# Batch 0's head of an attention-plus-MLP kernel in a new order: score halves of pairs 0 and 1 in a row, 54 narrow blank matmuls for six wide ones, and the first part of w_in loaded in two halves

## The chip, the cores and the metric

The kernel runs on one core of one Trainium2 chip. The metric is the device time of one execution in microseconds, taken as the median of three runs. The profile of the kernel before comes from one further execution.

## The reference, cut to what matters

```python
# q, k, v: (4 batches, 8 heads, 768 positions, 64)
k_sum = k.reshape(B, H, 24, 32, D).max(axis=3)        # one key per block of 32
v_sum = v.reshape(B, H, 24, 32, D).mean(axis=3)
scores_l = where(|i - j| < 16, q @ k.T / 8, -1e9)     # local window
scores_s = q @ k_sum.T / 8 + log(32)                  # 24 block summaries
a = softmax(concat([scores_l, scores_s], -1))
x = (a @ concat([v, v_sum], 2)).transpose(0, 2, 1, 3).reshape(3072, 512)
h = x @ w_in                                          # 512 x 2048
out = (h * sigmoid(beta * h)) @ w_out                 # 2048 x 512
```

## The kernel before, in words

The work goes batch by batch (B = 4). Within a batch the eight heads are four pairs g = 0 to 3, since two heads of 64 fill the 128 partitions. Attention of a pair runs in two halves u = 0, 1 of 384 positions: scores into PSUM, exponential on ScalarE, product with the values, division on VectorE, transposition to xT. Then comes the MLP: sixteen 128-row tiles of h = w_in.T x, SiLU on ScalarE, and the product with w_out. Attention of batch b + 1 is woven into the output product of batch b, so only batch 0's attention has no matrix work beside it. This is the **head**, and the change is there.

Every engine executes its instructions in the order of the program, and nothing reorders them. For the head that order is the list HEAD, one entry per step, read from left to right; a step puts instructions on one engine. The names:

- `blank n w`: n matmuls of zeros, w columns wide, each with its own 128x128 weight load, result unused (line 737).
- `kt g x`, `qt g x`: sixteen transpositions of pair g's keys or queries from the loaded rows into PSUM bank x (line 384; banks 0 to 5 are the halves of big0, big1, big2, banks 6 and 7 are one0 and one1). `kc g e`, `qc g e`: the copy to SBUF by engine e (a ScalarE, d VectorE, p GpSimd; the helpers are lines 368, 371 and 374).
- `km g`: maximum over key blocks on VectorE (line 361).
- `vc g e`: cast of the loaded values vst to ve (line 456); for pair 3 in two pieces. `vl`, `vu`: the lower and upper parts of the shifted copy vo. `sm x g..`: block means of the values by matmul (line 473); `mc g e`: their copy to vm_one.
- `sc g u bg`: the scores of pair g, half u, into big tile bg (lines 415 to 426, 18 matmuls). `ex g u`: their exponential on ScalarE (line 447).
- `av g x`: the product of half 0 with the values (lines 519 and 525); `no g`: division (lines 537, 538); `xt g x` and `xc g e`: transposition (line 545) and copy to xT.
- `wi i`: the load of columns 512 i to 512 i + 511 of w_in, cast on the way, issued by GpSimd (line 331). `begin p lo hi`: for h tiles 2p and 2p + 1 the matmuls of the contraction blocks lo to hi - 1 (line 578). `silu`: ScalarE's table switch.

Behind the head comes `main`, a list of steps of TensorE with side steps at positions given by the table AT: `h_two` finishes the h tiles of half 0, `av_two` does half 1 of the value product (line 511), eight GpSimd copies `v_odd` (lines 463, 464) fill the rest of vo, then GpSimd issues the loads of batch 1's keys, w_out (four parts) and batch 1's queries. VectorE scales w_out by 1/beta as its parts land (line 337).

Loads of batch 0: the keys and queries come in six pieces through GpSimd's queue (line 195). The values of pair 0 are loaded at once by SyncE; those of pairs 1 to 3 (line 216) wait until the third piece of keys has landed. Matmuls of line 384, 415 and so on are each preceded by a weight load in the same instruction stream.

Of the kernel before, what the change touches and what calls it, by code (L numbers as in the profile page):

```python
# [81 lines left out]
}  # L82

HEAD = [
# [12 lines left out]
]  # L97

FIRST = [('k', 0, 2), ('k', 2, 4), ('k', 4, 8), ('q', 0, 2), ('q', 2, 4), ('q', 4, 8)]
# [3 lines left out]
def kernel(  # L103
# [10 lines left out]
    nc = tc.nc  # L114
# [25 lines left out]
    k1 = d_model // P  # L140
# [73 lines left out]
    def load_v0(g):  # L214
        src = pair(v, 0, g)
        return nc.sync.dma_start(out=vst[g][:], in_=bass.AP(src.tensor, src.offset - W * D,
                                                            [[D, P], [P * D, JV], [1, D]]))

    def behind(a, b):
        tc.add_manual_dep(a.ins, b.ins.name,  # L220
                          mybir.DependencyInfo(mybir.DependencyClass.Sync, mybir.DependencyReason.DATA),
                          reason="order of loads")
# [8 lines left out]
    blank = head.tile([P, 512], bf16, name="blank")  # L231
# [27 lines left out]
    km = [const.tile([P, P], bf16, name=f"km{g}") for g in range(G)]  # L259
# [26 lines left out]
    vl = [None] + [load_v0(g) for g in range(1, G)]  # L286
# [28 lines left out]
    w_in_sb = const.tile([P, k1, d_ff], bf16, name="w_in_sb")  # L315
# [11 lines left out]

    w_in_r = moe_w_in.rearrange("(a p) n -> p a n", p=P)
    w_out_r = moe_w_out.rearrange("(a p) n -> p a n", p=P)
    def load_w_in(lo, hi):  # L330
        return nc.gpsimd.dma_start(out=w_in_sb[:, :, lo:hi], in_=w_in_r[:, :, lo:hi])

    def load_w_out(i, n=4):
        return nc.gpsimd.dma_start(out=w_out_sb[:, n * i:n * i + n], in_=w_out_r[:, n * i:n * i + n])
# [477 lines left out]
        cp(*a)  # L812

    def w_in_part(i):
        x = load_w_in(512 * i, 512 * i + 512)
        if i == 0 and HOLD[2] is not None:
            behind(x, (vl[1:] + rows0)[HOLD[2]])

# [2 lines left out]
            "ex": lambda g, u: weigh(0, g, u), "vc": lambda g, e, lo=0, hi=JV: v_cast(eng_of(e), g, lo, hi),  # L821
            "vu": upper, "vl": lower, "av": av0, "no": lambda g: norm(0, g, turns.pop(("o", g)), [0]),
            "xt": x0, "xc": x_copy, "wi": w_in_part, "silu": silu_table, "begin": begin}
    for name, *args in HEAD:
        STEP[name](*args)
# [145 lines left out]
```

## Time and profile before

| what | value |
|---|---|
| three runs | 209.53, 209.86, 211.06 us; median 209.86 |
| profiled execution: its time, its span | 210.59 us, 208.9 us |
| TensorE matmul busy | 200.0 us, 96% of the span |
| VectorE, ScalarE, GpSimd busy | 138.8, 124.9, 61.5 us |
| DMA | 34.12 MB, mean 163 GB/s |
| first h matmul (line 578) | 25.84 us after the span's start |

The span runs from the first to the last instruction; 1.69 us of the profiled execution lie around it. PE is TensorE's matmul row and PEld its weight loads, which overlap. In a row of the timeline stand the start, the busy time of the group, engine, line, operation, tiles and count, and in brackets how long the engine had been idle and what ended that. `issue` means that the profile shows nothing that the engine waited for.

### The profile page before, as it was taken

The page shows a single profiled execution, that of the slowest core. Times are in us where ns is not written, and L with a number is a line of the kernel's source. Part 1 is how long each engine was busy: PE and PEld are TensorE (multiplying, and loading weights), DVE is VectorE, ACT ScalarE, POOL GpSimd, SP SyncE. Part 2 cuts the span into 40 slices and gives each one's busy share as a digit, 9 for nine tenths or more (in the row PEclk, how much of TensorE's full clock was granted, in tenths as well). Part 3 has the DMA queues.
Part 4 walks back from the last instruction along what each step waited for, and adds up shares of the span by engine and source line. Part 5 has one row for each costly group of instructions (what it writes and reads, how often), then busy time and mean ns, then how long its engine had stood idle before and what let it go on. Part 6 is the DMA issues. An engine that isn't in the chain of part 4 may idle for free.

```text
span 208.9 us, 5772 instructions
## 1 busy us (share of the span) xinstructions
PE 200.0 (96%) x2383; PEld 138.9 (67%) x2387; DVE 138.8 (66%) x314; ACT 124.9 (60%) x189; POOL 61.5 (29%) x95
## 2 busy tenths in 40 slices
PE   7887899999999999999999999999999999999993
PEld 2476666665555675666888975667888856668882
DVE  4496674599999982868999621999889304464132
ACT  2365876679678212966979238768894439662210
POOL 7706991101530017422520162452501100000011
PEclk9999999999999999999999999999999999999998
DMA  5997999999958999999779979999936820000242
GB/s 114 188 221 124 167 208 207 206 207 222 184 139 222 218 246 260 225 188 209 148 173 250 199 213 285 205 192 202 122 126 66 189 100 3 0 0 3 100 100 100
DMA packets 79193, 34.12 MB, mean 163 GB/s; under 512 B 61488, under 2 KB 76224, under 8 KB 79168
## 3 DMA queue, kind: packets, MB, share of 16 engines
q1 hardware_dynamic: 61968, 23.92, 54.9%
q0 software_dynamic: 7424, 7.34, 22.0%
q10 hardware_dynamic: 9776, 2.50, 8.8%
q8 instruction: 18, 0.29, 0.6%
q14 instruction: 7, 0.06, 0.1%
HBM read 27.37 MB, written 6.29 MB: 161 GB/s over the span
## 4 chain that ended last, share of the span: by engine, by line
PE 78%; DMA 10%; DVE 6%; issue 2%; ACT 2%; POOL 1%; POOLq 0%
PE big L600 28%; PE one L664 16%; PE acc L664 12%; PE big L578 5%; DMA vst<-in_v_dram 4%; DMA w_in_sb<-in_moe_w_in_dram 4%; PE one L584 3%; DMA krow<-in_k_dram 3%; PE one L615 3%; PE one L600 2%; PE big L436 2%; PE big L511 2%; PE big L584 2%; PE big L384 1%; DVE xn L538 1%
## 5 line engine op out<-in xcount | busy, mean ns | idle before, releaser
L600 PE MATMUL big<-xT,w_in_sb 128*128 128x384 bf16 x360 | 60.5, 326 | 0.0
L600 PEld LDWEIGHTS <-w_in_sb 128*128 128x128 bf16 x384 | 37.6, 98 | 25.1 <-issue 0.7
L611 ACT ACTIVATE h_sb<-big,beta_sb 128x768 bf16<-128x768 f32 x45 | 39.6, 905 | 24.0 <-PE big L600 23.9
L664 PEld LDWEIGHTS <-h_sb 128*128 128x128 bf16 x320 | 30.6, 98 | 4.6 <-issue 0.2
L645 POOL TENSOR_TENSOR o_sb<-p,u 128x256 f32<-128x256 f32 x10 | 7.3, 728 | 84.8 <-DVE u L645 74.4
L447 ACT ACTIVATE e<-big,bias 128x768 bf16<-128x768 f32 x32 | 27.4, 900 | 6.7 <-PE big L426 4.3
L664 PE MATMUL one<-w_out_sb,h_sb 128*128 128x256 bf16 x240 | 30.4, 273 | 0.2 <-DVE u L645 0.2
L664 PEld LDWEIGHTS <-s_sb 128*128 128x128 bf16 x240 | 23.1, 98 | 3.3 <-issue 0.5
L645 DVE TENSOR_TENSOR s_sb<-h_sb 128x768 bf16<-128x768 bf16 (+2 forms) x16 | 7.8, 488 | 23.7 <-ACT h_sb L611 23.6
L645 DVE TENSOR_TENSOR u<-one,p 128x256 f32<-128x256 f32 x20 | 8.4, 419 | 17.4 <-PE one L664 17.4
L456 POOL CAST ve<-vst 128x832 bf16<-128x832 f32 (+2 forms) x16 | 14.5, 914 | 17.9 <-DMA vst<-in_v_dram 14.9
L615 PE MATMUL one<-w_out_sb,h_sb 128*128 128x512 bf16 x61 | 14.5, 380 | 0.4 <-issue 0.3
L451 DVE TENSOR_TENSOR e<-e,mask 128x768 bf16<-128x768 bf16 x24 | 14.1, 618 | 0.4 <-ACT e L447 0.2
L368 ACT COPY o_sb<-one 128x256 f32<-128x256 f32 (+1 forms) x14 | 6.1, 433 | 12.9 <-PE one L664 7.1
L365 POOL COPY kw<-km 128x288 bf16<-128x288 bf16 x12 | 6.4, 534 | 22.5 <-DVE km L357 12.2
L361 DVE TENSOR_REDUCE km<-kT 128x24 bf16<-128x768 bf16 x12 | 11.3, 944 | 2.1 <-ACT kT L368 2.1
L538 DVE TENSOR_TENSOR xn<-big,r 128x768 bf16<-128x768 f32 x12 | 11.5, 957 | 0.4
L578 PE MATMUL big<-xT,w_in_sb 128*128 128x384 bf16 x64 | 11.4, 326 | 0.3 <-DMA w_in_sb<-in_moe_w_in_dram 0.3
L664 PE MATMUL acc<-t_sb,h_sb 128*128 128x256 bf16 x80 | 10.9, 273 | 0.0
L368 ACT COPY p<-acc 128x256 f32<-128x256 f32 x10 | 3.8, 376 | 11.6 <-PE acc L664 7.3
L664 PE MATMUL one<-t_sb,s_sb 128*128 128x256 bf16 x80 | 10.4, 273 | 0.2 <-ACT o_sb L368 0.2
L831 ACT ACTIVATE h_sb<-big,beta_sb 128x384 bf16<-128x384 f32 x16 | 8.3, 578 | 3.7 <-PE big L578 3.7
(145 smaller groups left out, 315.0 us busy)
## 6 DMA issues: line engine op xcount, KB each, us to landing
out_dram<-o_sb SPq DMA_DIRECT2D x19, 256.0 KB, 3.5
vst<-in_v_dram SPq DMA_DIRECT2D x13, 336.0 KB, 5.2
kst<-in_k_dram SPq DMA_DIRECT2D x8, 384.0 KB, 4.8
qst<-in_q_dram SPq DMA_DIRECT2D x8, 384.0 KB, 4.5
w_in_sb<-in_moe_w_in_dram POOLq DMA_DIRECT2D x4, 512.0 KB, 8.9
w_out_sb<-in_moe_w_out_dram POOLq DMA_DIRECT2D x4, 512.0 KB, 14.2
vo<-ve SPq DMA_DIRECT2D x12, 107.2 KB, 2.6
vst<-in_v_dram SPq DMA_DIRECT2D x3, 416.0 KB, 8.9
```

The lines of the kernel that those rows point to most:

```text
L361: nc.vector.tensor_reduce(out=km[g][:, NK:NK + nb], in_=kT[g][:, W:W + S].rearrange("p (n f) -> p n f", f=block), op=ALU.max, axis=AX.X)
L447: nc.scalar.activation(out=e[:], in_=s[:, :, 0:HS], func=ACTF.Exp, bias=bias[:, 0:1], scale=scale)
L451: nc.vector.tensor_mul(out=e.rearrange("p h (m q) -> p h m q", q=QT), in0=e.rearrange("p h (m q) -> p h m q", q=QT), in1=(mask2 if b > 1 e ...
L456: eng.tensor_copy(out=ve[:, g, lo:hi, 0:D], in_=vst[g][:, lo:hi])
L538: nc.vector.tensor_mul(out=x[:, 3 * us[0]:3 * us[0] + 3 * n].rearrange("p (k j) h d -> p k (j h) d", k=n), in0=tv[:, :, :, 0:D], in1=r[:, ...
L578: nc.tensor.matmul(t[:, 0:HS], w_in_sb[:, ki, i * P:(i + 1) * P], xT[:, ki, 0:HS], start=(ki == 0), stop=(ki == k1 - 1))
L584: nc.tensor.matmul(t[:, 0:HS], w_in_sb[:, ki, i * P:(i + 1) * P], xT[:, ki, lo:lo + HS], start=(ki == 0), stop=(ki == k1 - 1))
L600: nc.tensor.matmul(o, w_in_sb[:, ki, i * P:(i + 1) * P], x, start=(ki == 0), stop=(ki == k1 - 1))
L611: nc.scalar.activation(out=o, in_=t, func=ACTF.Silu, scale=beta_sb[:, i:i + 1])
L615: nc.tensor.matmul(t[:, 0:hi - lo], h_sb[:, n, ms * P:(ms + 1) * P], w_out_sb[:, n, lo:hi], start=(n == 0), stop=(n == k2 - 1))
L645: eng.tensor_tensor(out=o, in0=a, in1=b, op=op)
L664: nc.tensor.matmul(SLOTS[n], a[:, j, t * P:(t + 1) * P], b[:, j], start=(j == 0 and n not in (2, 3, 7)), stop=(j == J2 - 1), skip_group_ch ...
```

## The change

The list HEAD is replaced by another order of nearly the same steps. The blank matmuls go from 10 + 2 + 4 + 2 of 512 columns to 10 + 2 of 512, 27 of 64, 27 of 64, and 1 of 512. Both halves of pairs 0 and 1 are now scored one behind another with pair 2's second half next, several copies go to other engines, and `wi 0` issues two DMAs, contraction blocks 0 and 1 first, then 2 and 3.

```diff
 HEAD = [
-    ('blank', 10, 512), ('beta',), ('blank', 2, 512), ('kt', 0, 3), ('blank', 4, 512), ('kc', 0, 'a'), ('kt', 1, 6),
...
+    ('blank', 10, 512), ('beta',), ('blank', 2, 512), ('kt', 0, 3), ('blank', 27, 64), ('kc', 0, 'a'), ('kt', 1, 6),
...
-    def load_w_in(lo, hi):
-        return nc.gpsimd.dma_start(out=w_in_sb[:, :, lo:hi], in_=w_in_r[:, :, lo:hi])
+    def load_w_in(lo, hi, a=0, b=k1):
+        return nc.gpsimd.dma_start(out=w_in_sb[:, a:b, lo:hi], in_=w_in_r[:, a:b, lo:hi])
...
     def w_in_part(i):
-        x = load_w_in(512 * i, 512 * i + 512)
+        x = load_w_in(512 * i, 512 * i + 512, 0, k1 // 2 if i == 0 else k1)
+        if i == 0:
+            load_w_in(0, 512, k1 // 2, k1)
```

GpSimd, from the cast of pair 1's values to the first v_odd copy (vst_92, vst_93 and vst_94 are the values of pairs 1, 2 and 3). Before:

```order
L456 CAST ve<-vst_92 128x13x64
L331 DMA w_in_sb<-in_moe_w_in_dram 128x4x512
L374 COPY vo<-ve 32x2x3x64
L374 COPY vo<-ve 64x2x3x64
L331 DMA w_in_sb<-in_moe_w_in_dram 128x4x512
L456 CAST ve<-vst_94 128x7x64
L456 CAST ve<-vst_94 128x6x64
L331 DMA w_in_sb<-in_moe_w_in_dram 128x4x512 x2
L463 COPY vo<-ve 64x2x3x64
```

Now:

```order
L456 CAST ve<-vst_92 128x13x64
L331 DMA w_in_sb<-in_moe_w_in_dram 128x2x512 x2
L331 DMA w_in_sb<-in_moe_w_in_dram 128x4x512
L374 COPY vo<-ve 64x2x3x64
L456 CAST ve<-vst_93 128x13x64
L456 CAST ve<-vst_94 128x7x64
L331 DMA w_in_sb<-in_moe_w_in_dram 128x4x512
L374 COPY vo<-ve 64x2x3x64
L331 DMA w_in_sb<-in_moe_w_in_dram 128x4x512
L463 COPY vo<-ve 64x2x3x64
```

Three issues now stand in a row, GpSimd casts pair 2 as well (VectorE did), and pair 2's upper copy stands between the third and fourth column parts.

TensorE, around its row 447 (counted over matmuls and weight loads from the program's start; kT_123 and kT_124 are the keys of pairs 0 and 1, qn_177 to qn_179 the queries of pairs 0 to 2, km_129 the block maxima of pair 2, and big_85, big_80, big_81 are big0, big1, big2). Before, the end of `sc 0 1` and the start of `sc 2 0`:

```order
L422 LDWEIGHTS kT_123
L422 MATMUL big_80<-qn_177,kT_123 96x64
L426 LDWEIGHTS edge
L426 MATMUL big_80<-identity,edge 128x64
L426 LDWEIGHTS edge
L426 MATMUL big_80<-identity,edge 128x64
L415 LDWEIGHTS km_129
L415 MATMUL big_81<-qn_179,km_129 128x384
```

Now, the end of `sc 1 1` and the start of `qt 2`:

```order
L422 LDWEIGHTS kT_124
L422 MATMUL big_85<-qn_178,kT_124 96x64
L426 LDWEIGHTS edge
L426 MATMUL big_85<-identity,edge 128x64
L426 LDWEIGHTS edge
L426 MATMUL big_85<-identity,edge 128x64
L384 LDWEIGHTS qrow
L384 MATMUL one_78<-identity,qrow 64x96
```

At the same count of instructions TensorE now stands earlier in the head's work: the queries of pairs 2 and 3 and the first value product are still ahead of it, because 98 more rows lie before.

22 rows, old and new, of the table HEAD are left out of this document.

## The prediction

> **What bounds the kernel now.** I read the stages first, as a table of windows of the span: length, then busy time and instruction count of PE, PEld, DVE, ACT, POOL, then the granted clock, DMA share and GB/s.
>
> ```profile
> 0.00:16.20 16.20, 13.71 (x221) 7.91 (x223) 10.19 (x42) 6.45 (x8) 7.86 (x20) 1.00 1.02 176
> 16.20:17.45 1.25, 0.00 (x0) 0.00 (x0) 1.03 (x2) 0.00 (x0) 0.13 (x1) 1.00 1.28 231
> 17.45:25.80 8.35, 7.60 (x178) 6.05 (x177) 5.10 (x13) 6.92 (x10) 7.98 (x14) 1.00 0.88 127
> 25.80:58.50 32.70, 32.59 (x390) 19.73 (x391) 26.04 (x68) 24.38 (x42) 11.43 (x19) 1.00 1.18 204
> 58.50:75.90 17.40, 16.69 (x261) 10.40 (x256) 16.48 (x32) 9.00 (x14) 1.37 (x2) 1.00 0.99 192
> ```
>
> From 25.80 to 58.50 us TensorE is idle for 0.11 us, so a later or earlier start there is passed on. From 58.50 to 75.90 both TensorE (16.69 of 17.40) and VectorE (16.48) are nearly full. Only the first 25.8 us can be changed by a new order: TensorE is idle there for 16.20 - 13.71 + 1.25 + 0.75 = 4.5 us, but part of its busy time is blanks. Next the chain of waits in order of time, for what ends the head.
>
> ```profile
> 9.44 7.76 DMA vst<-in_v_dram
> ...
> 18.14 7.65 DMA w_in_sb<-in_moe_w_in_dram
> ...
> 25.84 0.82 PE big L578 x4
> ...
> 28.78 0.50 PE one L511 x24
> ```
>
> Pair 1's values land at 17.2, GpSimd casts them, only then does it issue w_in's first part, which lands 7.65 us later at 25.79, and the first h matmul waits for that. How much does it wait? The timeline of TensorE:
>
> ```profile
> 20.60 0.34 PE L415 MATMUL big<-qn,km 64*128 64x384 bf16 x2
> 21.31 0.34 PE L545 MATMUL one<-identity,xn 128*128 128x128 bf16 x3
> ...
> 22.30 0.57 PE L473 MATMUL one<-ve,A_avg 128*32 128x128 bf16 x14
> 23.26 0.35 PE L519 MATMUL one<-vm_one,e 128*128 128x65 bf16 x6 [0.39 <-DVE vm_one L371]
> ...
> 25.84 0.82 PE L578 MATMUL big<-xT,w_in_sb 128*128 128x384 bf16 x4 [0.33 <-DMA w_in_sb<-in_moe_w_in_dram]
> ...
> 26.67 2.11 PE L578 MATMUL big<-xT,w_in_sb 128*128 128x384 bf16 x12
> 28.71 0.22 PE L511 MATMUL one<-ve,e 128*64 128x65 bf16 x1
> ```
>
> Only 0.33 us: behind the landing of pair 1 TensorE is itself busy almost without a gap. So halving w_in's first part can give 0.33 us by itself, and more only if the work before it gets shorter too.
>
> **The change part by part.** *Blanks.* The price of each kind:
>
> ```profile
> 7.09 1.04 PE L737 MATMUL one<-blank 128*128 128x512 bf16 x4
> 8.06 0.53 PE L384 MATMUL one<-identity,krow 96*64 96x96 bf16 x16
> ...
> 14.07 0.87 PE L384 MATMUL big<-identity,qrow 96*64 96x96 bf16 x32
> 14.87 0.36 PE L519 MATMUL one<-vm_one,e 128*128 128x65 bf16 x6
> 15.16 0.22 PE L525 MATMUL one<-ve,e 96*64 96x65 bf16 x1
> ...
> 15.47 0.34 PE L415 MATMUL big<-qn,km 64*128 64x384 bf16 x2
> ```
>
> Four wide blanks take 7.09 to 8.06, so 0.97 us. No narrow blank is in the trace; the nearest row is the value product of line 519, also a 128x128 weight load before each 65-column matmul: six from 14.87 to 15.16, 0.048 us each. From below the columns alone bound it, 1.04 / 4 x 64 / 512 = 0.03; from above a weight load that overlaps nothing, 0.098 as in the next row, plus that 0.03.
>
> ```profile
> L600 PEld LDWEIGHTS <-w_in_sb 128*128 128x128 bf16 x384 | 37.6, 98 | 25.1 <-issue 0.7
> ```
>
> I take 0.05: 1.35 us for a group of 27. Thirty-two transpositions take 14.07 to 14.87, so `kt` or `qt` costs 0.40, a value product 14.87 to 15.47, 0.60, and a score set 20.60 to 21.31, 0.71. TensorE's new row, from 7.09: blanks to 8.44, `kt 1` 8.84, blanks 10.19, `sm 0` (the fourteen of pairs 2 and 3 take 0.57 above; I take 0.38 for these seven) 10.57, `kt 2` 10.97, one wide blank 11.2, `qt 0` and `kt 3` 12.0. There ScalarE decides, by these rows:
>
> ```profile
> 8.63 0.80 ACT L368 COPY kT<-one 128x768 bf16<-128x768 bf16 x1 [0.63 <-PE one L384]
> ...
> 20.55 0.51 ACT L368 COPY vo<-ve 64x384 bf16<-64x384 bf16 x1
> ```
>
> It now does `mc 0` (a smaller copy, 0.3 by estimate from the second row), `vu 0` (0.51), `kc 2` and `qc 0` (0.80 each) in a row from 10.75 on, to about 13.1, and pair 0's scores wait for the last. Three score sets end at 15.2, then `qt 2`, `av 0`, `qt 3`, `sc 1 0` and `sc 2 1` (2.8 us) bring TensorE to 18.0, just as the cast of pair 1 ends at 18.14. So the later start of pairs 2 and 3 is covered by the wait for the values.
>
> *GpSimd*, which everything behind 17.3 hangs on:
>
> ```profile
> 2.70 1.35 POOL L195 DMA_DIRECT2D krow<-in_k_dram  x2
> ...
> 17.32 0.88 POOL L456 CAST ve<-vst 128x832 bf16<-128x832 f32 x1 [7.95 <-DMA vst<-in_v_dram]
> 18.14 0.76 POOL L331 DMA_DIRECT2D w_in_sb<-in_moe_w_in_dram  x1
> 18.94 1.05 POOL L374 COPY vo<-ve 32x384 bf16<-32x384 bf16 x2
> 19.93 0.74 POOL L331 DMA_DIRECT2D w_in_sb<-in_moe_w_in_dram  x1
> 20.72 1.01 POOL L456 CAST ve<-vst 128x448 bf16<-128x448 f32 x2
> 21.67 1.48 POOL L331 DMA_DIRECT2D w_in_sb<-in_moe_w_in_dram  x2
> 23.20 0.50 POOL L463 COPY vo<-ve 64x384 bf16<-64x384 bf16 x1
> ...
> 27.51 0.79 POOL L195 DMA_DIRECT2D krow<-in_k_dram  x1
> ```
>
> An issue of half size costs between 0.67 (the two smaller key loads, 1.35 / 2) and 0.76; I take 0.70. New: two halves 18.14 to 19.54, second part to 20.3, `vu 1` (0.5) 20.85, cast of pair 2 (0.88) 21.7, seven of thirteen columns of pair 3 (0.48) 22.2, third part 23.0, `vu 2` 23.5, fourth part 24.25, then eight v_odd copies (27.51 - 23.20 = 4.3) to 28.55. So on TensorE `av 1` waits for `vu 1` until 20.85, when `sm 1` (0.38), `xt 0` (0.3; three transpositions have 0.34 in the row at 21.31, with their tail) and two score sets have been done since 20.2: a first cover of 0.65 us. `av 1` ends at 21.45, and the block means of pairs 2 and 3 start at 22.25 instead of 22.30: a second cover, 0.8, so that TensorE could be **1.4 us late** at 18.1 and lose nothing. `av 2` starts at 23.5 instead of 23.26. But `sc 3 0` now stands before it, under that wait, where `sc 3 1` (0.71) stood behind it. `av 2`, `xt 1` and `av 3` (0.60 + 0.3 + 0.60, the division of pair 2 beside `av 3`) end at 25.0, `xt 2` at 25.3: the first h matmul at **25.35 instead of 25.84**, if half of w_in's first part is there. The second half is needed at 26.0, and the whole landed at 25.79 before. From there to line 511 the same 16 matmuls and one transposition stand, 28.71 - 25.84 = 2.87 us: 28.2. Pair 1's v_odd copy, the eighth, ends at 28.55, where line 511 would need it at 28.45 (pair 0's half of the 0.50 in the chain's last row): 0.1 is lost. TensorE is **0.4 us ahead**. Loads of batch 1 are issued 1.05 us later (28.55 for 27.51); this is hidden if w_in's 2 MB keep the queue busy past 30, and costs w_out up to 1.05 us if not (the queue's rate is below).
>
> *What it is worth later.* VectorE's timeline:
>
> ```profile
> 39.85 1.14 DVE L337 TENSOR_SCALAR w_out_sb<-w_out_sb,inv_beta 128x512 bf16<-128x512 bf16 x4 [1.68 <-DMA w_out_sb<-in_moe_w_out_dram]
> ...
> 57.70 2.85 DVE L451 TENSOR_TENSOR e<-e,mask 128x768 bf16<-128x768 bf16 x3
> ```
>
> VectorE waits until 39.85 for w_out's first part and has no gap worth naming from there into the masks at 57.70. An earlier TensorE shortens 58.50 to 75.90 only as far as this landing moves forward as well. It follows w_in through one queue, which stalled:
>
> ```profile
> q0 software_dynamic: 166, 0.15, 95.9%
> q0 software_dynamic: 1189, 1.19, 121.0%
> ```
>
> These are the queue's rows for 22.5 to 24.0 and for 24.0 to 30.0: 0.15 MB in 1.5 us against 0.20 MB per us. At that rate w_in's 2 MB last ten us from about 20 on, so that the later issues behind it are hidden. Three issues in a row may close that gap (0.75 us) or not. I take half of the 0.4 us as passed on.
>
> **The sum.** 210.59 for the profiled execution less 0.2; the runs' median stands 0.73 lower, so 209.86 - 0.2, in round numbers **209.6**.
>
> **The rivals.** *The instruction block comes late (slower).* Between 16.20 and 17.45 TensorE ran nothing, in the midst of twelve like matmuls:
>
> ```profile
> 17.50 0.23 PE L422 MATMUL big<-qn,kT 64*96 64x64 bf16 x2 [1.32 <-issue]
> q8 instruction: 1, 0.02, 5.5%
> ```
>
> The second row is the instruction queue from 14.7 to 16.2: one block of code, which takes 5.5% of 16 x 1.5 us = 1.3 us on one DMA engine, when 444 matmuls and weight loads have run (221 + 223 in the first window). I read the idle time as a wait for it. In the new order that row falls at the end of `sc 1 1`, needed at 15.2. If the block is usable no earlier than 17.5, the steps behind it move by 2.3 us; 1.4 of that are covered, and TensorE is 0.5 us behind before instead of 0.4 ahead: 210.4. It decides from 16.6 on (15.2 + 1.4). For it: nothing in the change makes the block lighter. Against: the 98 extra rows run without waits at 7 to 10 us, so the block is asked for earlier.
> [...]
>
> *Narrow blanks cost their full weight load (slower).* At 0.10 us each the work behind them comes 54 x 0.05 = 2.7 us later, of which 1.4 are covered; less the lead of 0.4 that is 0.9 behind before, 210.8. At the upper bound of 0.128 it is 4.2 - 1.8 = 2.4, so 212.3. It decides from 0.083 on.
>
> *The loads run earlier (faster).* The block of 1.3 us sat on one DMA engine among the values' packets. If it is read before them, and if that engine is the one by which pair 1's values landed at 17.2, then cast, w_in and w_out move up to 1.3 us forward together, and with them both limits of the later stage: 208.5; with the queue's gap of 0.75 us closed too, 207.8.
>
> *The halves do nothing*: both lie in one queue; if the second lands no sooner than 25.79 and the order alone is slower than I worked out, 209.9 to 210.2.
>
> **Chances.** Forecast 0.45 (209.4 to 209.9), useless halves 0.12, late block 0.18, dear narrow blanks 0.08, earlier loads 0.17. About 1%, 2.1 us, is what a measurement of this kernel can tell from no change; only the far ends of the cases pass it, a third of the earlier loads (0.06) and most of the dear blanks (0.06). The range leaves these out: from 208.1, past the earlier loads' 208.5, to 211.2, past the late block and the dear blanks at 0.10.
>
> **What would show it.** Right: the first h matmul at 25.2 to 25.5 without a wait for w_in; line 737's 64-column group 1.3 to 1.5 us per 27; idle time at TensorE before 18 us no longer inside one score set, or ended before 16.5. Wrong: a gap marked issue at 15.2 that lasts to 17; line 511 after 28.8; w_out's first scaling (39.85) more than 0.8 us away from where it was.

## The result, and the profile after

The changed kernel takes 211.25 us, median of 20 runs (210.14 to 212.55). The kernel before takes 209.98 in 20 runs beside it (209.01 to 211.83). The ratio is 1.0058, 95% interval 1.0039 to 1.0078: **1.2 us slower**, where 0.2 us faster was forecast.

The profiled execution of the changed kernel took 210.53 us (span 208.8), 0.7 below its median, and the one of the kernel before 210.59, 0.6 above its own. These two show the mechanism, not its size. The stages first, in the columns of the table before.

```profile
0.00:16.20 16.20, 14.20 (x277) 9.16 (x279) 8.45 (x39) 8.52 (x11) 7.86 (x20) 1.00 1.01 174
16.20:17.45 1.25, 1.25 (x38) 1.06 (x35) 1.22 (x4) 0.58 (x1) 1.25 (x2) 1.00 0.96 218
17.45:25.80 8.35, 7.42 (x149) 5.66 (x150) 5.35 (x15) 5.93 (x10) 7.99 (x14) 1.00 1.04 163
25.80:58.50 32.70, 32.15 (x385) 19.16 (x383) 26.44 (x67) 23.99 (x42) 12.19 (x19) 1.00 1.18 195
58.50:75.90 17.40, 16.40 (x252) 10.17 (x250) 15.86 (x31) 8.32 (x14) 1.61 (x2) 1.00 0.98 207
```

The hole of 1.25 us at 16.20 is gone. From 25.80 to 58.50, where TensorE was idle for 0.11 us, it is now idle for 0.55, and the last column, what the DMA engines moved, has fallen from 204 to 195 GB/s. TensorE's timeline at the places that the prediction named:

```profile
6.80 0.96 PE L737 MATMUL one<-blank 128*128 128x64 bf16 x27
7.69 0.53 PE L384 MATMUL one<-identity,krow 96*64 96x96 bf16 x16
...
14.50 0.20 PE L426 MATMUL big<-identity,edge 64*128 64x64 bf16 x2 [0.21 <-issue]
...
24.30 1.22 PE L578 MATMUL big<-xT,w_in_sb 128*128 128x384 bf16 x6
...
50.97 1.55 PE L384 MATMUL big<-identity,qrow 96*64 96x96 bf16 x64 [0.44 <-DMA qrow<-in_q_dram]
60.16 0.56 PE L486 MATMUL big<-ve,A_avg 128*32 128x128 bf16 x25 [0.20 <-POOL ve L456]
```

A narrow group lasts from 6.80 to 7.69, 0.033 us per blank. The wait marked issue stands where it was expected and lasts 0.21 us. The first h matmul starts at 24.30 instead of 25.84, without a wait. But the queries of batch 1 and the block means of its values (line 486) now make TensorE wait, as nothing did before. GpSimd's timeline shows what was issued when:

```profile
16.20 0.88 POOL L456 CAST ve<-vst 128x832 bf16<-128x832 f32 x1 [6.83 <-DMA vst<-in_v_dram]
17.03 2.17 POOL L331 DMA_DIRECT2D w_in_sb<-in_moe_w_in_dram  x3
...
27.64 0.79 POOL L195 DMA_DIRECT2D krow<-in_k_dram  x1
28.43 2.99 POOL L334 DMA_DIRECT2D w_out_sb<-in_moe_w_out_dram  x4
```

Pair 1's values came 1.1 us earlier than in the first profile of before (cast at 16.20 instead of 17.32), and krow(1) still left 0.13 us later. Counted from GpSimd's first issue of w_in, which takes out when the values happened to land, the first h matmul stands 7.27 us behind it (before: 25.84 - 18.14 = 7.70) and krow(1), the load of batch 1's keys, 10.61 (before 9.37). VectorE's timeline, and the chain of waits where it leaves TensorE:

```profile
39.22 1.14 DVE L337 TENSOR_SCALAR w_out_sb<-w_out_sb,inv_beta 128x512 bf16<-128x512 bf16 x4 [2.23 <-DMA w_out_sb<-in_moe_w_out_dram]
```

```profile
38.73 0.77 PE big L584 x4
39.50 0.86 DVE w_out_sb L337 x3
...
51.85 5.70 DMA vst<-in_v_dram
...
77.80 1.30 PE big L600 x8
```

VectorE waits 2.23 us for w_out's first part instead of 1.68. The chain enters VectorE's scaling at 39.50, 0.28 behind this landing (it names TensorE's line 584 as the step before), and runs over VectorE and the loads of batch 1 to the first h matmuls of batch 1 (line 600), where nothing is left of the lead (before: 77.94 in the chain). From the first matmul of line 600 to the end all profiles of this study have the same 131.0 to 131.3 us.

### The profile page after: what moved, and what is told of

Same layout as the page of the kernel before. It is cut to its first block, busy times and chain, and to the rows that moved or that the text cites. A ratio compares the mean times of both kernels' runs of the same rounds, so it can differ in the third digit from the quotient of the medians.

```text
span 208.8 us, 5871 instructions
## 1 busy us (share of the span) xinstructions
PE 200.7 (96%) x2436; PEld 140.1 (67%) x2436; DVE 137.0 (66%) x312; ACT 125.4 (60%) x191; POOL 64.3 (31%) x96
## 4 chain that ended last, share of the span: by engine, by line
PE 67%; DVE 10%; DMA 9%; POOL 7%; issue 2%; ACT 2%; SPq 1%; ACTq 0%; POOLq 0%
PE big L600 28%; PE one L664 16%; PE acc L664 12%; DMA vst<-in_v_dram 6%; PE big L578 4%; DMA krow<-in_k_dram 3%; DVE kw L371 2%; POOL ve L456 2%; PE one L600 2%; DVE s_sb L645 2%; PE big L511 2%; POOL w_in_sb L331 2%; PE big L436 1%; POOL vo L463 1%; POOL vo L464 1%
## 5 line engine op out<-in xcount | busy, mean ns | idle before, releaser
L456 POOL CAST ve<-vst 128x832 bf16<-128x832 f32 (+1 forms) x16 | 15.6, 988 | 13.8 <-DMA vst<-in_v_dram 10.6
L615 PE MATMUL one<-w_out_sb,h_sb 128*128 128x512 bf16 x64 | 15.0, 380 | 0.0
L538 DVE TENSOR_TENSOR xn<-big,r 128x768 bf16<-128x768 f32 (+1 forms) x13 | 12.1, 927 | 0.4
L568 POOL CAST qn<-qst 128x768 bf16<-128x768 f32 x8 | 7.6, 962 | 9.3 <-DMA qst<-in_q_dram 5.4
```

The lines of the kernel that those rows point to most:

```text
L456: eng.tensor_copy(out=ve[:, g, lo:hi, 0:D], in_=vst[g][:, lo:hi])
L538: nc.vector.tensor_mul(out=x[:, 3 * us[0]:3 * us[0] + 3 * n].rearrange("p (k j) h d -> p k (j h) d", k=n), in0=tv[:, :, :, 0:D], in1=r[:, ...
L615: nc.tensor.matmul(t[:, 0:hi - lo], h_sb[:, n, ms * P:(ms + 1) * P], w_out_sb[:, n, lo:hi], start=(n == 0), stop=(n == k2 - 1))
```

## The experiments

"W" is the start of GpSimd's first issue of w_in. "Whole" means w_in's first part in one load, "mid" krow(1) issued in the middle of the v_odd copies. The profile columns are from one execution each, the times from 12 runs against 23 to 36 of the kernel before (the changed kernel's first row: 20 each).

| kernel | median us | ratio to before, 95% | W | first h matmul - W | krow(1) issue - W |
|---|---|---|---|---|---|
| before, first profile | 209.98 | | 18.14 | 7.70 | 9.37 |
| before, second | 209.88 | 0.996 to 1.002 | 16.43 | 7.89 | 9.57 |
| changed | 211.25 | 1.004 to 1.008 | 17.03 | 7.27 | 10.61 |
| changed, again | 211.24 | 1.001 to 1.007 | 17.44 | 7.43 | 10.78 |
| wide blanks | 210.94 | 1.001 to 1.007 | 16.31 | 7.92 | 10.64 |
| before, narrow blanks | 210.32 | 0.998 to 1.004 | 17.77 | 7.64 | 9.44 |
| whole first part | 209.74 | 0.993 to 0.999 | 17.27 | 6.73 | 10.06 |
| whole, again | 209.96 | 0.998 to 1.002 | 17.58 | 6.73 | 10.06 |
| whole, cast for issue | 210.89 | 1.000 to 1.007 | 17.05 | 7.28 | 10.63 |
| before, halves | 210.24 | 0.996 to 1.002 | 17.27 | 7.95 | 10.13 |
| krow(1) before v_odd | 210.85 | 0.999 to 1.005 | 17.29 | 7.27 | 6.09 |
| same, whole | 210.11 | 0.996 to 1.002 | 16.96 | 6.73 | 5.54 |
| whole, late cast | 210.48 | 0.999 to 1.003 | 17.63 | 6.73 | 10.88 |
| krow(1) mid v_odd | 210.02 | 0.997 to 1.002 | 17.34 | 7.40 | 8.37 |
| same, whole | 209.49 | 0.994 to 0.999 | 17.46 | 7.23 | 7.68 |
| same, whole, again | 209.23 | 0.993 to 0.999 | 17.41 | 7.23 | 7.68 |
| same, whole, w_out early | 209.47 | 0.994 to 0.999 | 17.93 | 6.76 | 7.73 |
| v_odd order only | 211.20 | 1.003 to 1.010 | 17.62 | 7.38 | 10.77 |
| whole, late loads | 211.10 | 1.002 to 1.009 | 17.53 | 6.72 | 11.78 |
| before, krow(1) mid | 210.09 | 0.996 to 1.003 | 16.82 | 8.45 | 7.37 |

**Which part of the change costs?** The changed kernel once more, and it with one part undone or done alone:

> The changed kernel once more, unaltered, for a second profile and as the measure of its three neighbours. In its first profile the head was 1.54 us ahead (first h matmul 24.30 instead of 25.84) and nothing of it was left at 77.80, where the first tile of batch 1's h matmuls starts (before 77.78); that one execution was at the fast end of its runs, and the median of all stands 1.27 us over the kernel before. Theory A (instruction blocks: 98 more rows on TensorE shift every later block border): a second profile shows issue gaps at places other than before. Theory B (loads: the loads of batch 1 and what waits for them swallow the lead, and land at a different time from run to run): the waits for krow(1), w_out, qrow(1) or the values are longer than before in the slower runs. Both expect 1.0 to 1.5 us over the kernel before.

```diff
-('blank', 27, 64) ... ('blank', 27, 64)
+('blank', 4, 512) ... ('blank', 2, 512)
```

> The changed kernel with the old six wide blanks (4 and 2 of 512 columns) in place of the 54 narrow ones; order and halves as changed. By its profile 27 narrow blanks take 0.89 us and four wide ones 0.97, two 0.49, so the head's TensorE work is 0.3 us shorter. Theory A (the 98 extra rows cost by where later code blocks begin): back to the kernel before, within 0.4 us. Theory B (loads): stays 0.9 to 1.5 us over the kernel before.

The reverse of this edit, in the kernel before:

> The kernel before with its six wide blanks replaced by 54 narrow ones, order and single first part of w_in as before. Theory A: 0.9 to 1.5 us slower than the kernel before, with an issue gap where it had none, and the gap of 1.32 us at 16.2 moved into another place of the head. Theory B: within 0.4 us of the kernel before, since the loads leave when they did.

```diff
-        x = load_w_in(512 * i, 512 * i + 512, 0, k1 // 2 if i == 0 else k1)
-        if i == 0:
-            load_w_in(0, 512, k1 // 2, k1)
+        x = load_w_in(512 * i, 512 * i + 512)
```

> The changed kernel with w_in's first part in one load again. The halves landed at 21.63 and 23.99, and the first h matmul started at 24.30; the whole would land near 23.6 to 24.0, so the head itself changes by under 0.3 us. GpSimd has one issue less, about 0.7 us, ahead of the cast of pair 2. Theories A and B both expect it within 0.4 us of the changed kernel; if the halves are the cause (one load more in GpSimd's queue delays krow(1), w_out and the values), it is 0.9 us or more below the changed kernel.

Wide blanks stay slow (210.94), and narrow ones in the kernel before (210.32) can't be told from no change: the 98 extra rows are not the cause, and theory A falls. The whole first part takes 209.74 and 209.96, so **the two halves cost 1.4 us**, which neither theory had expected. They buy nothing; TensorE's and GpSimd's timelines of the first run with the whole part:

```profile
24.00 1.22 PE L578 MATMUL big<-xT,w_in_sb 128*128 128x384 bf16 x6
```

```profile
17.27 1.50 POOL L331 DMA_DIRECT2D w_in_sb<-in_moe_w_in_dram  x2
...
27.33 0.79 POOL L195 DMA_DIRECT2D krow<-in_k_dram  x1
```

The first h matmul does not wait for the whole part either, and it comes earlier: 6.73 us behind W. One issue less on GpSimd brings pair 1's copy, the casts of pairs 2 and 3 and krow(1) forward (krow(1) 10.06 us behind W instead of 10.61). In the second profile of the changed kernel (211.93 us), TensorE waits longer still for a load of batch 1:

```profile
52.67 1.51 PE L384 MATMUL big<-identity,qrow 96*64 96x96 bf16 x62 [1.56 <-DMA qrow<-in_q_dram]
```

**The split, or GpSimd's time?** An idle cast in the issue's place, krow(1) ahead of the v_odd copies with halves and with the whole part, and halves in the kernel before:

```diff
+        if i == 0:
+            nc.gpsimd.tensor_copy(out=h_sb[:, k2 - 1, 0:10 * D]..., in_=vst[0][:, 0:10])
```

> The changed kernel with w_in's first part whole, and on GpSimd, in the place of the second half's issue, a cast of ten columns of pair 0's staged values into a part of h_sb that is overwritten later (0.88 us x 10 / 13 = 0.68 us, against 0.70 for the issue). It computes nothing that is used. Theory G (the halves cost because one issue more on GpSimd makes krow(1) and all loads behind it later, while the queue has run dry): as slow as the changed kernel, 210.8 to 211.5. Theory S (the split itself costs, as one more transfer in the queue or by what waits for it): as fast as the kernel with the whole part, 209.4 to 210.1.

```diff
-('wi', 3), ('xt', 2, 4)
+('wi', 3), ('kr',), ('xt', 2, 4)      # 'kr' issues krow(1); more_loads no longer does
```

> The changed kernel with both halves, but krow(1) issued right behind w_in's fourth part, ahead of GpSimd's eight v_odd copies (at 23.1 instead of 27.6; the copies and w_out's four issues 0.8 later). Its profiles show the software queue less than full from 29.5 to 31.5, between w_in's last part and krow(1). Theory G: the dip goes, krow(1) lands 0.5 us or more earlier, w_out and qrow(1) with it, 1.0 us or more below the changed kernel: 209.4 to 210.3. Against it stand the v_odd copies, 0.8 us later ahead of the line-511 products, which would show as a wait there for vo. Theory S: 210.8 or more.

> The same with w_in's first part whole. Theory G: the dip is 0.5 us smaller to begin with, so at most as fast as both remedies together: 208.7 to 209.7. Theory S: 209.4 to 210.1, unless the late v_odd copies cost 0.5 us.

> The kernel before with w_in's first part in two halves and nothing else. There GpSimd's first issue of w_in comes at 18.1 and the queue is full from 24.0 to past 33, so krow(1) issued at 28.2 instead of 27.5 is still in time. Theory G: within 0.4 us of the kernel before. Theory S: 1.2 to 1.8 us slower than it.

The cast (0.73 us) gives 210.89, and W to first h matmul and to krow(1) are those of the halves' first profile within 0.02: it is GpSimd's time. The halves in the kernel before cost nothing that can be told (210.24): there w_in's last part lands 15.5 us behind W (in the changed kernel 14.7), so that krow(1), 10.13 us behind W, still finds the stream running (207 GB/s from 29 to 39 us). Moving krow(1) ahead of all copies brought less than expected: 210.85 and 210.11. TensorE's timeline of the first of these shows a wait in line 511, and VectorE's that the copies, now 0.8 us later, bring it in:

```profile
28.43 0.19 PE L511 MATMUL one<-ve,e 128*64 128x65 bf16 x1 [0.55 <-DVE ve L480]
28.79 0.19 PE L511 MATMUL one<-vo,e 128*64 128x65 bf16 x1 [0.17 <-POOL vo L464]
```

```profile
28.12 0.26 DVE L480 COPY ve<-vm_one 32x384 bf16<-32x384 bf16 x1 [0.46 <-POOL vo L463]
```

**Head or loads?** The cast behind w_in's fourth part; then krow(1) in the middle of the copies:

> w_in's first part whole, and the 0.68 us cast on GpSimd (of no use, as in the run with the busy engine) not behind w_in's first part but behind its fourth, just ahead of the v_odd copies. The head's own waits for GpSimd (upper copies, casts of pairs 2 and 3) are then not delayed, the v_odd copies and batch 1's loads are. Theory G-late (what costs is the later v_odd copies and loads): 210.6 to 211.3, as with the cast up front. Theory G-head (what costs is the later head, which feeds all that follows): 209.5 to 210.1, as with the whole part alone.

```diff
-    'first': [-2.097, 0.853, -1.457, 0.459, ...    # v_odd of pairs 0, 1, 2, 3
-    'loads': [2.306],                              # krow(1), w_out, qrow(1)
+    'first': [-2.097, -2.0, -1.457, 0.459, ...
+    'loads': [-1.9, 2.306],                        # krow(1) / w_out, qrow(1)
```

> The changed kernel with both halves; on GpSimd the v_odd copies of pairs 0 and 1 first, then the issue of krow(1), then the v_odd copies of pairs 2 and 3, which are needed only at the second group of line-511 products 4 us later, then w_out and qrow(1). krow(1) is issued near 25.5 instead of 27.6 and no first line-511 product waits for vo, as it did for 0.55 and 0.17 us when krow(1) stood ahead of all eight copies. Theory G-late: 209.6 to 210.2, 1 us below the changed kernel. Theory G-head: 210.6 or more.

> The same order on GpSimd with w_in's first part whole: a candidate to beat both kernels. Theory G-late: 208.9 to 209.6. Theory G-head: 209.4 to 210.0, no change against the whole part alone, 209.74.

> The changed kernel with w_in's first part whole once more, for a second profile (the first was of the slowest of its runs) and a tighter figure: 209.5 to 210.1 by every theory. A profile of a run below 209.7 should start batch 1's h matmuls at 76.8 or earlier instead of 77.95, since from there to the end all profiles so far have the same 131.1 us within 0.1.

The late cast costs 0.6 us (210.48), its line-511 wait included. That lies between what the two theories expected, so neither holds alone. krow(1) in the middle brings the kernel with halves to 210.02, and with the whole part to 209.49.

**Copies or loads?** That edit also moved pair 1's copy ahead. Its two parts apart, and two controls:

```diff
-    'first': [-2.097, 0.853, -1.457, 0.459, ...
+    'first': [-2.097, -2.0, -1.457, 0.459, ...     # 'loads' as in the changed kernel
```

> The changed kernel, both halves, with GpSimd's v_odd copies in the order of pairs 0, 1, 2, 3 instead of 0, 2, 3, 1; krow(1) and the other loads leave behind all eight copies, as in the changed kernel (10.6 us behind w_in's first issue). Theory V (line 511 waits for pair 1's copy, and TensorE carries that on): 209.8 to 210.4, like the run with krow(1) in the middle. Theory L (batch 1's loads leave late): 210.8 to 211.4, no change, though line 511 no longer waits.

```diff
+        for _ in range(2):                         # in more_loads, ahead of krow(1)
+            nc.gpsimd.tensor_copy(out=h_sb[:, k2 - 1, 0:10 * D]..., in_=vst[0][:, 0:10])
```

> The changed kernel with w_in's first part whole, and two casts of 0.68 us (of no use, into a part of h_sb that is overwritten later) on GpSimd behind the v_odd copies, right ahead of krow(1). The head and line 511 are as with the whole part alone (209.7 to 210.0); only batch 1's loads leave 1.36 us later, 11.4 us behind w_in's first issue instead of 10.06. Theory L: 210.8 to 211.4. Theory V: 209.6 to 210.2.

> The kernel before, unaltered, for a second profile. If the first one showed a run with late values, w_in's first issue now starts at 17.2 to 17.8 instead of 18.14, the first h matmul 7.6 to 8.0 us behind it, krow(1) 9.4 behind it, and the h matmuls of batch 1 start 131.1 us ahead of the end. Time 209.7 to 210.3.

> The kernel before with GpSimd's order of the fastest run so far: v_odd of pairs 0 and 1, krow(1), v_odd of pairs 2 and 3, the other loads. If the loads alone set the time of this stage, it comes to the same 209.5 as the new order with it, and the new order of the head is worth nothing; if the head's 1 us ahead counts as well, it stays at 209.8 to 210.3, since its queue was full until past 33 anyway.

This settles copies or loads. The order of the copies alone does nothing (211.20), and holding back the loads alone costs 1.25 us against the whole part's mean of 209.85 (211.10). The programs at 211.20 and 210.02 differ only in whether GpSimd issues krow(1) behind all copies or in their middle. In the first, the chain of waits goes from krow(1)'s issue over the loads to line 600:

```profile
28.44 0.73 POOL krow L195
29.18 10.27 DMA w_out_sb<-in_moe_w_out_dram
...
39.74 0.87 DVE w_out_sb L337 x3
...
54.52 4.64 DMA vst<-in_v_dram
...
78.26 1.30 PE big L600 x8
```

In the second it stays on TensorE from 24.90 to 60.15, with no load in it, and reaches line 600 at 77.06, 1.2 us earlier. The windows of the two, 29 to 33 and 33 to 39 us, in the same order:

```profile
29.00:33.00 4.00, 4.00 (x47) 2.42 (x46) 1.93 (x7) 3.27 (x7) 3.96 (x6) 1.00 1.15 181
33.00:39.00 6.00, 6.00 (x74) 4.00 (x72) 3.13 (x20) 3.98 (x9) 0.97 (x2) 1.00 1.19 186
```

```profile
29.00:33.00 4.00, 4.00 (x47) 2.43 (x45) 1.90 (x7) 3.10 (x7) 3.73 (x6) 1.00 1.24 207
33.00:39.00 6.00, 6.00 (x73) 3.97 (x72) 3.57 (x23) 3.98 (x9) 0.97 (x2) 1.00 1.24 206
```

And GpSimd's queue in the same two profiles over these ten us (packets, MB, share):

```profile
q0 software_dynamic: 1821, 1.82, 116.5%
```

```profile
q0 software_dynamic: 2046, 2.04, 123.4%
```

0.22 MB are missing, at 0.206 MB per us **1.1 us of transfer**. VectorE's first scaling of w_out follows 1.0 us later (0.7 if both are counted from W), in the same order:

```profile
39.47 1.14 DVE L337 TENSOR_SCALAR w_out_sb<-w_out_sb,inv_beta 128x512 bf16<-128x512 bf16 x4 [2.07 <-DMA w_out_sb<-in_moe_w_out_dram]
```

```profile
38.47 1.14 DVE L337 TENSOR_SCALAR w_out_sb<-w_out_sb,inv_beta 128x512 bf16<-128x512 bf16 x4 [1.16 <-DMA w_out_sb<-in_moe_w_out_dram]
```

Why the queue starves shows best where the loads were held back: GpSimd's issue, and the rate of all DMA from 29 to 33 us in 40 slices of 0.1 us (0.49 of its 0.51 MB are this queue's).

```profile
29.31 0.79 POOL L195 DMA_DIRECT2D krow<-in_k_dram  x1
```

```profile
GB/s 205 184 225 205 287 174 215 205 195 154 297 51 31 10 10 20 10 10 72 82 92 31 20 61 82 61 51 61 82 82 154 133 184 195 205 154 225 205 215 184
```

w_in's stream breaks off at 30.1. krow(1) has been under issue since 29.31, yet the rate rises at 30.8, 1.5 us behind the issue's start, and is full only from 32.0 to 32.3 on, 2.7 to 3.0 behind it. Here the issue would have had to start at least that long before the queue ran dry. This trace does not show which packet is the first of krow(1); the rate's first rise stands 0.7 us behind the end of the issue and 1.5 behind its start, and the full rate comes another 1.2 to 1.5 us later.

In two more traces 3 us were too little; the rate from 29 to 39 us in slices of 0.25, first the changed kernel's first profile, then the second one of the kernel before:

```profile
GB/s 213 197 229 209 246 143 143 131 156 164 176 172 172 201 193 180 143 156 188 209 197 168 143 127 147 180 176 164 152 193 197 209 205 197 209 209 217 201 205 201
```

```profile
GB/s 201 152 164 184 176 193 193 201 197 205 197 213 209 201 213 201 201 242 152 193 184 209 201 193 221 201 197 197 188 205 205 209 213 205 205 205 209 197 213 213
```

In the first, krow(1) is issued at 27.64, the rate falls at 30.25, 2.6 us later, and is back at 200 only 4.6 us behind the issue. In the second it is issued at 26.00, and there is a small dip 3.25 us later.

The second profile of the kernel before, timelines of GpSimd, TensorE and VectorE:

```profile
16.43 0.76 POOL L331 DMA_DIRECT2D w_in_sb<-in_moe_w_in_dram  x1
...
26.00 0.79 POOL L195 DMA_DIRECT2D krow<-in_k_dram  x1
```

```profile
16.57 0.23 PE L422 MATMUL big<-qn,kT 64*96 64x64 bf16 x2 [0.31 <-issue]
...
24.32 0.81 PE L578 MATMUL big<-xT,w_in_sb 128*128 128x384 bf16 x4
```

```profile
37.57 1.16 DVE L337 TENSOR_SCALAR w_out_sb<-w_out_sb,inv_beta 128x512 bf16<-128x512 bf16 x4 [0.79 <-DMA w_out_sb<-in_moe_w_out_dram]
```

The values had come 1.7 us earlier, the wait marked issue was 0.31 us instead of 1.32, the first h matmul did not wait for w_in, and it stood at 24.32, where the changed kernel has 24.30. The first profile was of a run with late values: its W is the latest of all twenty profiles. In the kernel before, an early krow(1) wins nothing (210.09), where the queue is full or nearly so without it (2.05 and 1.96 MB from 29 to 39 us in its two profiles). By the expectation this also says that the new order of the head is worth something once the loads are in time, since with the same early krow(1) and one whole first part it takes 209.49.

**How far it goes.** w_out's first part too ahead of the last copies, and the fastest version once more:

> The fastest version so far (new order, w_in's first part whole, krow(1) ahead of the v_odd copies of pairs 2 and 3) with w_out's first part issued there too. Its profile shows VectorE waiting 1.02 us for that part, until 38.29, and the queue nearly full all along, so that w_out's first part cannot land much earlier: 209.2 to 209.7, no change that can be measured. If the first scaling starts 0.4 us or more earlier, and the time with it, the queue was not the limit.

> The fastest version so far once more, unaltered: 209.2 to 209.8, 0.2 to 0.8 us below the kernel before.

The further issue changes nothing (209.47, ratio 0.994 to 0.999), as expected if the queue itself is the limit. The new order with one whole first part and krow(1) in the middle of the copies takes 209.49 and 209.23, 0.7 and 0.8 us below the runs of the kernel before beside it (210.17 and 210.00), and **beats both kernels**.

## Why the prediction was wrong, step by step

- **The step that failed** is the sentence "Loads of batch 1 are issued 1.05 us later; this is hidden if w_in's 2 MB keep the queue busy past 30". The lateness was sized right: krow(1) leaves 10.61 us behind W instead of 9.37 or 9.57, 1.0 to 1.2 more. The condition was met: in the changed kernel's profile the rate holds until 30.25, and w_in's last part, issued at 22.39, lands 9.3 us later, at 31.7. Hidden the lateness was not all the same. I compared the issue, 28.55, with the end of the transfer before it, 30, and left out the way from issue to full rate, 2.7 to 3.0 us in the trace with the loads held back. The other branch ("costs w_out up to 1.05 us if not") stood in the text but got no chance of its own; with the 0.2 us of gain taken off, it gives 210.7, nearer to the result.
- **TensorE 0.4 us ahead**: right. Counted from W, 7.27 and 7.43 against 7.70 and 7.89, so 0.3 to 0.6. As forecast, it is of use only as far as w_out's landing moves forward, and this moved back: 22.19 us behind W instead of 21.14 (37.57 - 16.43) in the second profile of before, 21.71 in the first. Line 511 waits 0.3 us for pair 1's copy (27.46 to 27.75) where 0.1 was forecast; this costs nothing that can be told, since the run without this wait takes 211.20.
- **The first half of w_in is needed at 25.35**: a useless step. The whole part was there in time as well, 5.3 and 6.1 us behind its issue, and the wait of 0.33 us that the halves were to remove is not there in the second profile of before. The rival "the halves do nothing" was right that they buy nothing, though not for its reason (the second half landed 7.0 us behind W, sooner than the whole part's 7.65 in the first profile), and it gave them no price; the issue of 0.70 us that I had put into GpSimd's row costs 1.4.
- **Narrow blanks**: 0.033 us each, not 0.05, at the lower bound, so their weight loads, 27 within 0.84 us, overlap; that rival falls. That nothing reorders an engine's instructions is what the first profile of before shows for VectorE, ScalarE and GpSimd: the lines of their 314, 189 and 95 instructions stand in the program's order. It does not hold for weight loads: in the same profile, from 9.46 to 9.535 us, six weight loads of line 384 have started and four matmuls, though each load stands right before its own matmul in the program.
- **The instruction block**: a wait marked issue stands where I said, at 14.50, with 0.21 us, so that rival falls too; in the fourteen profiles of the new order with the narrow blanks it is never above 0.61. I leaned too much on one profile, though 1.32 was not alone: 0.98 us are marked so with wide blanks in the new order, 0.96 in the old order with krow(1) in the middle. That these waits are for a block of code was not tried: seventeen of the twenty traces have at most 0.61 us so marked, three have 0.96 to 1.32.
- **Earlier loads**: they did not come. W lies between 16.43 and 18.14 in the five profiles of the old order and between 16.31 and 17.93 in the fifteen of the new, with a mean of 17.3 in both.
- **Reading one profile**: the later stages were sized from a run whose values came late. There w_in's stream began late, stalled at 22.5 to 24.0 and ended at 33.42, so that krow(1) had room to spare, which made the 1.05 us look safe.

What stays open is how the halves' 1.4 us divide. Loads held back by 1.72 us cost 1.25, so by that slope the halves' 0.55 us on krow(1) are worth 0.4; the remaining 1.0 would fall to the first h matmul, 0.54 later. The late cast points the same way: its krow(1), 10.88 us behind W, is later than with halves, its first h matmul is not, and it costs only 0.6. Against that, krow(1) alone wins 1.2 back, and the fastest version has its first h matmul 7.23 us behind W, as late as with halves. So late loads are needed for the loss, since moving krow(1) forward removes it, but how it divides between them and the later head is not shown. Nor do the missing packets alone give the time: from 29 to 39 us the changed kernel's queue moved 1810, the whole part's two profiles 1842 and 1855, and these took 210.53, 210.68 and 209.96 us.

## What to carry to other kernels

Ask of an issue not only whether it starts before the queue runs dry, but by how much: here the way from issue to full rate took 2.7 to 3.0 us in one trace and 4.6 in another. So when work in front of the queue gets shorter, move the loads behind it forward too. Count what each instruction on the issuing engine adds to the loads behind it: here the split transfer's second issue (0.71 us) and a cast in its place (0.73) put krow(1) 0.55 and 0.57 us later. And try the next load ahead of work that is not needed soon: here krow(1) ahead of the last four v_odd copies took 1.2 us off the time with halves (211.25 to 210.02). Before sizing a stage from one profile, count from an event inside the run, as W here, or take a second profile.

## What the runs showed of the hardware that was not expected

- From the start of a GpSimd issue to the full rate of a queue that has run dry: 2.7 to 3.0 us in one trace (29.31 to 32.0 and 32.3), and to the first rise 1.5 us. In another trace, where the rate only fell to between 131 and 176 GB/s, it was back at 200 4.6 us behind the issue (27.64 to 32.25).
- After such a hole the queue was not at once full again: with krow(1) late the DMA engines moved 186 GB/s even from 33 to 39 us, 206 with krow(1) in time. The cause of this second loss was not tried.
- The landing of pair 1's values, and with it W, differed between the two profiled executions of the kernel before by 1.7 us (18.14 and 16.43), more than the 1.2 us that the change costs.
- A 64-column blank with its own 128x128 weight load took 0.033 us (27 from 6.80 to 7.69); an eighth of a wide one's 0.24 (0.97 us for four) is 0.030.
